# Loading part of w4 to sixteen partitions, and the last V quad with V moving, in a one-core decode block

## The chip, the core and the metric

The kernel runs on one core of a Trainium2 chip. The metric is device time in microseconds (us) of one execution; the median of three runs is given. The core has TensorE (PE; its weight loads are shown as PEld), VectorE (DVE), ScalarE (ACT), GpSimd (POOL) and SyncE (SP), which issues nearly all DMA loads here. Sixteen DMA engines move the data.

## The reference

One decode step for eight sequences (B = 8, S = 1, D = 512): attention over a window of a cache, then an MLP block, each with its residual.

```python
W = min(4096, max(256, Sk // 4))                       # 2048 of Sk = 8192
q = (layernorm(x) @ wq).reshape(B, 1, 32, 128)
k, v = the last W positions of the caches, 8 heads, each used by 4 query heads
o = softmax(q @ k^T * 128**-0.5) @ v
h = x + o.reshape(B, 1, 4096) @ wo

x = layernorm(h)
hs = token shifts of gelu(layernorm(x) @ w1) @ w2      # for S == 1 the shifts leave only zeros
x1 = x + hs
h2 = h + x1 + gelu(layernorm(x1) @ w3) @ w4            # w3: 512 x 1792, w4: 1792 x 512
```

Since S is 1, the shifted branch is zero, and w1 and w2 are not read. What is read: wq and wo (4 MB each), 32 quads of K and V (2 MB each), w3 and w4 (1.75 MB each), some 79 MB in all.

## The kernel before

Every engine has a list of operations, written out in order by the program (class `Engine`); an operation waits for the semaphore counts that it names, and counts its own engine's semaphore up. Nothing is reordered.

**The stream of loads.** `loads` lists them in order: for each sequence b and half j of the heads a K quad `("k", b, j)`, and two sequences later the V quad `("v", b, j)`, then wo in four parts, then w3 in two and w4 in four. SP issues all of them in this order. A quad is 128 partitions of 16 KB in a slot of `ring`, which has eight slots (`NS`); a load waits until the quad that held its slot has been used (`taken`). w3 lies in the slot of K quad (7, 0), w4 in that of V quad (5, 0). w4's 1792 rows are put on the 128 partitions in groups of 8, 3, 2 and 1 rows per partition (`w4_chunks`, `w4_ends`), each with a load and a semaphore of its own. FC is 14, the number of 128-row chunks of w4, and FH, 8, the number in the first group.

**Attention.** `pe_T` transposes a quarter of a K quad into `kT_ps`, ACT and DVE copy it to `kT_sb` (`evict`, L334 and L336), `pe_QK` multiplies (L345). `softmax_1` to `softmax_5` take a sequence's scores to `pT_sb`; the products with `mask_b` (L384) that spread the probabilities over head groups run on GpSimd (for the last sequence half of them on DVE). `pe_PV(i)` multiplies quarter r of V quad w = i // 4. In its form `moving` (L445) V streams through the array and the probabilities are the weights; the result holds four head groups side by side, and only a part of each is wanted: `pick_part` and `pick_rest` (L480, L483) select and add these in four steps, the first on ACT for late quads and the others on DVE, and `finish(w)` sums them with one product (L496) and scales them into `oT_all` (`scale`, L435). In its form `held` (L454), used only for the last quad (w = 15), V is the weights, 64 products accumulate the wanted result straight into `S_ps[1]`, and `scale` follows at once. NV is 15, the number of quads in the form `moving`; OWN gives quads NV - 3 and NV - 2 (12 and 13) PSUM banks of their own, and SHARE (10) is the number of quads that are picked in the main loop.

**The tail.** `reorder` (L534, L539, L540) turns `oT_all` into `oR`; `pe_wo` (L548) multiplies with the four parts of wo as they arrive. `stream(n)` (L596) is n products of 512 columns into `O2_ps` that nobody reads; such products stand between several steps. Then come the layernorm statistics (L685 to L700) and `uT` (L692), the input of w3. `pe_w3` (L710) multiplies w3 by `uT` in two halves, as its two loads arrive: eight chunks with 64 moving columns into `y_ps[0]`, six with 32 into `y_ps[1]`. DVE multiplies with `r2` (L738), ACT applies gelu (L741), `pe_fin` (L747, through `rows`) puts the residual into `z_ps`, and `pe_w4` (L755) adds the 14 chunks of w4, each as a pair of products on the two column halves, waiting for the arrival of each group. Then the copies (L775, L776) and the store.

Of the kernel before, what the change touches and what calls it, by code (L numbers as in the profile page):

```python
# [6 lines left out]
dt = mybir.dt  # L7
ACT = mybir.ActivationFunctionType
# [59 lines left out]
def bass_sequential_preLN__sliding_block_cached__mixer_s_mlp__decode_kernel(  # L68
# [23 lines left out]
    with es:  # L92
# [98 lines left out]
        sem_wo = [S(f"sem_wo{i}") for i in range(NWO)]  # L191
        sem_x, sem_wq, sem_out = (S(n) for n in ("sem_x", "sem_wq", "sem_out"))
        sem_w3 = [S(f"sem_w3{i}") for i in range(2)]
        sem_w4 = [S(f"sem_w4{i}") for i in range(4)]
# [109 lines left out]
        def landed(l, cq):  # L304
            n = place[l]
            return sem_r[n % NS], 16 * (n // NS + 1)
# [1 line left out]
        e_Tlo, e_Thi, e_lo, e_hi, e_QK, e_PV = {}, {}, {}, {}, {}, {}  # L308
        e_sp, e_max, e_mT, e_neg, e_negps, e_negc, e_exp, e_PT, e_pT, e_lsel, e_Lb, e_rL, e_scale = ({} for _ in range(13))
        NG = NB * 8  # L310
        NV = 2 * NB - 1
        LAST = NB - 1

        def split(i):
# [112 lines left out]
        OWN = {NV - 3: kbank[0], NV - 2: kbank[2]}  # L427
        banks = [O_ps[:, :], O2_ps[:, :]]

        def bank(w):  # L430
            return OWN[w] if w in OWN else banks[0] if w > NV - 2 else banks[w % 2]

        def scale(b, j, src, *waits):
            hh = slice(16 * j, 16 * (j + 1))
            e_scale[b, j] = DV.op(lambda e: e.tensor_tensor(oT_all[:, hh, b], src, rL[:, b % 4, hh], ALU.mult),  # L435
                                  e_rL[b], *waits)

        def pe_PV(i):
            b, j, r = split(i)
            s, w = place["v", b, j] % NS, i // 4  # L440

            def moving(e):
                for c in range(4 * r, 4 * r + 4):
                    t = c % 2
                    ins = e.matmul(bank(w)[64 * t:64 * (t + 1), :], pT_sb[:, b % NB3, c, 64 * j:64 * (j + 1)],  # L445
                                   ring[:, s, :].rearrange("p (a c d) -> p c a d", a=4, c=16)[:, c],
                                   start=(c < 2), stop=(c >= 14), tile_position=(0, 64 * t), skip_group_check=True)
                return ins

            def held(e):  # L450
                for c in range(16):
                    n = 16 * r + c
                    lo = 128 * c + 64 * j + 16 * r
                    ins = e.matmul(S_ps[1][:, 0:32], ring[:, s, n * DH:(n + 1) * DH],  # L454
                                   pT_sb[:, b % NB3:b % NB3 + 2].rearrange("p u c n -> p (u c n)")[:, lo:lo + 32],
                                   start=(n == 0), stop=(n == NCQ - 1))
                return ins

            if w >= NV:
                e_PV[i] = PE.op(held, landed(("v", b, j), r), e_pT[b, 3])  # L460
                taken["v", b, j] = e_PV[i]
                return
            if w in OWN:
                free = [e_lo[NG - 1], e_hi[NG - 1], e_lo[NG - 2], e_hi[NG - 2]]
            else:
                free = [e_acc[NV - 5]] if w == NV - 1 else [e_acc[w - 2] if w > 1 else None, e_xp[0]]
# [7 lines left out]
        SHARE = NV - 5  # L474
        e_part = {}

        def pick_part(w, a, eng):
# [9 lines left out]
        def pick_rest(w, *parts):  # L487
            for a in parts:
                pick_part(w, a, DV)
                if a == 3:  # L490
                    e_acc[w] = e_part[w]

        def finish(w):
            b, j = w // 2, w % 2
            hh = slice(16 * j, 16 * (j + 1))
            e_oT[w] = PE.op(lambda e: e.matmul(oT_ps[:, hh], acc[w % 3][:, :], sum_f[:, :], start=True, stop=True),  # L496
                            e_acc[w], e_sum, small[0])
            scale(b, j, oT_ps[:, hh], e_oT[w])
            small[0] = e_scale[b, j]
# [57 lines left out]
        def pv(*quarters):  # L557
            for i in quarters:
                pe_PV(i)
                if i in at:  # L560
                    finish(at[i])
                if i == NG - 1:
                    scale(LAST, 1, S_ps[1][:, 0:16], e_PV[i])

        def scores(p):
            if 0 <= p - LQK < NG:
# [26 lines left out]
        def stream(n):  # L593
            def f(e):
                for _ in range(n):
                    ins = e.matmul(O2_ps[:, :], ident_b[:, :], kT_sb[:, (NG - 1) % NKT, 0:512], start=True, stop=True)  # L596
                return ins
            if n:
                PE.op(f, e_acc[NV - 4])

        def over_exp():
            pv(49)
# [38 lines left out]
        pv(60)  # L641
        finish(14)
        pv(61, 62, 63)

        e_oR = reorder()
        stream(3)
# [19 lines left out]


        w_free = [taken[quads[n - NS]] for n in (len(quads), len(quads) + 1)]
        for a, sem in enumerate(sem_w3):
            dma(SP, w3_sb[:, 2 * a:2 * (a + 1), :].rearrange("p r f -> p (r f)"),  # L670
                B_w3[256 * a:256 * (a + 1), :].rearrange("(p r) f -> p (r f)", r=2), sem, w_free[0])

        FH = 8
        w4_chunks, w4_ends, f0 = [], [], 0
        for r, sem in zip((8, 3, 2, 1), sem_w4):
            lo = len(w4_chunks)
            w4_chunks += [slice(f0 + i, f0 + 128 * r, r) for i in range(r)]
            dma(SP, w4_sb[:, lo:lo + r, :].rearrange("p r n -> p (r n)"),
                B_w4[f0:f0 + 128 * r, :].rearrange("(p r) n -> p (r n)", r=r), sem, w_free[1] if lo == 0 else None)
            w4_ends.append(lo + r)  # L680
            f0 += 128 * r
        assert len(w4_chunks) == FC
# [22 lines left out]
        def pe_w3(half, lo, hi, *waits):  # L705
            def f(e):
                for fc in range(lo, hi):
                    n, f = divmod(fc, FH)
                    for kc in (2 * half, 2 * half + 1):
                        ins = e.matmul(y_ps[n][:, f * NY[n]:(f + 1) * NY[n]], w3_sb[:, kc, w4_chunks[fc]],  # L710
                                       uT[:, kc, 0:NY[n]], start=(kc == 0 and f == 0), stop=(kc == KC - 1),
                                       skip_group_check=True)
# [17 lines left out]
        def bcf(t, n):  # L730
            a = t[:, :]
            return bass.AP(tensor=a.tensor, offset=a.offset, ap=[a.ap[0], [0, n], [1, B]])

        e_gT = []
        for n in range(2):
            fn = (FH, FC - FH)[n]
            cs = slice(n * FH * B, (n * FH + fn) * B)
            e = DV.op(lambda e, n=n, cs=cs, fn=fn: e.tensor_tensor(v3(g_x[:, cs]),   # L738
                y_ps[n][:, 0:fn * NY[n]].rearrange("p (f w) -> p f w", w=NY[n])[:, :, 0:B], bcf(r2, fn),
                                                                   ALU.mult), e_y[n], e_r2)  # L740
            e_gT.append(AC.op(lambda e, cs=cs: e.activation(gT[:, cs], g_x[:, cs], ACT.Gelu_apprx_tanh), e))  # L741
        z_ps = S_ps[1]

        def rows(e, w, rhs, start=False, stop=False):
# [6 lines left out]
        def pe_w4(lo, hi, *waits):  # L751
            def f(e):
                for fc in range(lo, hi):
                    for a in range(2):
                        ins = e.matmul(z_ps[64 * a:64 * a + B, 0:256], gT[:, fc * B:(fc + 1) * B],  # L755
                                       w4_sb[:, fc, 256 * a:256 * (a + 1)].rearrange("p (j r) -> p r j", r=2),
                                       start=False, stop=(fc == FC - 1), tile_position=(0, 64 * a), skip_group_check=True)
                return ins
            return PE.op(f, *waits)

# [52 lines left out]
```

## Time and profile before

| | us |
|---|---|
| median of three runs (193.4 to 193.74) | 193.5 |
| the profiled execution | 193.76 |
| its span, first to last instruction | 192.3 |
| DMA busy share of the chain that ended last | 78% |
| PE, DVE, ACT, POOL busy in the span | 159.8, 103.8, 84.4, 35.8 |

The granted TensorE clock is 1.0 throughout. HBM reads are 79.18 MB, 412 GB/s over the span. The profile is a page on one execution, with a trace behind it that answers questions: a timeline of instructions, who waited for whom, groups by line, and the records of single DMA packets and semaphore arrivals. Times in a timeline count from the start of the span. A line number in it is that of the code above.

The timeline gives busy stretches as "start, length, engine, line, operation, output<-inputs, sizes, count", and in brackets how long the engine had been idle and who released it.

### The profile page before, as it was taken

Reading aid. Unit: us, or ns where it says so; the run is one execution under the profiler, and the core shown is the slowest. Engines: PE = TensorE matmul, PEld = TensorE weight load, DVE = VectorE, ACT = ScalarE, POOL = GpSimd, SP = SyncE. Lnnn points to the kernel's source line nnn. Section 1 sums busy time; section 2 is a strip of 40 time slices with the busy share of each in tenths; the row PEclk is TensorE's granted clock in tenths of the full one; section 3 lists DMA queues with packets and bytes.
Section 4 is the critical chain, followed back from the end, with each engine's and each line's share of the span. In section 5 each row is a group of like instructions: output and inputs, shape, how many; then the busy total and the mean of one; then the engine's idle time right before and its main releaser. Section 6 shows DMA issues by size and latency. Waiting matters only on the chain.

```text
span 192.3 us, 4741 instructions
## 1 busy us (share of the span) xinstructions
PE 159.8 (83%) x2108; PEld 101.8 (53%) x2108; DVE 103.8 (54%) x256; ACT 84.4 (44%) x102; POOL 35.8 (19%) x44
## 2 busy tenths in 40 slices
PE   0028999789998989998999797979998998898795
PEld 0015767567665555655656464646565653366472
DVE  7702656367457654665475546554765456552050
ACT  5002776946744544454444532454445423530040
POOL 8000000350520080008000800052004402400000
PEclk9999999999999999999999999999999999999999
DMA  6999999999999999999999999999999999999992
GB/s 220 436 423 436 433 416 433 426 428 423 436 429 433 429 433 423 426 429 431 433 423 433 429 433 429 429 433 426 424 426 429 429 433 433 423 416 430 418 381 77
DMA packets 6244, 79.47 MB, mean 413 GB/s; under 512 B 705, under 2 KB 849, under 8 KB 1361
## 3 DMA queue, kind: packets, MB, share of 16 engines
q1 hardware_dynamic: 6208, 79.18, 97.0%
q8 instruction: 16, 0.26, 0.5%
q10 hardware_dynamic: 16, 0.01, 0.0%
q14 instruction: 4, 0.02, 0.0%
HBM read 79.18 MB, written 0.01 MB: 412 GB/s over the span
## 4 chain that ended last, share of the span: by engine, by line
DMA 78%; PE 16%; DVE 2%; SPq 2%; issue 1%; ACT 0%
DMA ring<-in_A_k_cache_dram 63%; DMA ring<-in_B_w_dram 16%; PE kT_ps L325 8%; PE O_ps L445 3%; PE S_ps L345 3%; SPq L199 2%; DVE kT_sb L336 1%; PE sm L394 1%; PE sm L496 1%; DVE pT_sb L407 1%; PE S_ps L755 0%; DVE mcol L356 0%; ACT P_sb L775 0%; PE sm L360 0%; PE sm L370 0%
## 5 line engine op out<-in xcount | busy, mean ns | idle before, releaser
L334 ACT ACTIVATE kT_sb<-kT_ps 128x1024 bf16<-128x1024 bf16 x64 | 65.2, 1023 | 65.4 <-PE kT_ps L325 65.4
L325 PE MATMUL kT_ps<-ident_p,ring 128*128 128x128 bf16 x1024 | 68.3, 220 | 9.0 <-DMA ring<-in_A_k_cache_dram 7.6
L336 DVE COPY kT_sb<-kT_ps 128x1024 bf16<-128x1024 bf16 x64 | 44.3, 692 | 48.9 <-PE kT_ps L325 48.9
L325 PEld LDWEIGHTS kT_ps<-ident_p,ring 128*128 128x128 bf16 x1024 | 57.7, 98 | 22.5 <-DMA ring<-in_A_k_cache_dram 10.5
L384 POOL TENSOR_TENSOR P_sb<-P_sb,mask_b 128x512 bf16<-128x512 bf16 x30 | 31.2, 1070 | 129.2 <-ACT P_sb L374 120.1
L445 PE MATMUL O_ps<-ring,pT_sb 128*64 128x512 bf16 x208 | 31.6, 390 | 0.0
L345 PE MATMUL S_ps<-kT_sb,qwin 128*32 128x512 bf16 x256 | 26.0, 390 | 0.0
L345 PEld LDWEIGHTS S_ps<-kT_sb,qwin 128*32 128x32 bf16 x256 | 6.8, 93 | 16.3 <-issue 14.4
L394 PE MATMUL sm<-ident_s,P_sb 128*128 128x128 bf16 x120 | 11.6, 219 | 2.0 <-DVE pT_sb L407 0.7
L407 DVE COPY pT_sb<-sm 128x512 bf16<-128x512 bf16 x28 | 11.6, 415 | 1.1 <-PE sm L394 1.1
L445 PEld LDWEIGHTS O_ps<-ring,pT_sb 128*64 128x64 bf16 x208 | 7.7, 108 | 6.1 <-issue 1.6
L394 PEld LDWEIGHTS sm<-ident_s,P_sb 128*128 128x128 bf16 x120 | 7.7, 97 | 4.5 <-issue 3.6
L480 DVE SCALAR_TENSOR_TENSOR acc<-O_ps,own_f,acc 128x128 f32<-128x128 f32 x24 | 8.4, 350 | 0.8
L268 PE MATMUL S_ps<-wbig,xlnT 128*32 128x512 bf16 x32 | 3.4, 596 | 5.3 <-DMA wbig<-in_A_wq_dram 5.3
L374 ACT ACTIVATE P_sb<-S_ps,negcol 128x512 bf16<-128x512 f32 x8 | 5.5, 687 | 3.0 <-DVE negcol L373 3.0
L254 PE MATMUL sm<-ident_b,xln_b 8*128 8x8 bf16 x4 | 0.3, 174 | 7.6 <-DVE xln_b L223 7.6
L496 PEld LDWEIGHTS sm<-sum_f,acc 128*128 128x128 f32 x20 | 3.0, 188 | 6.3 <-DVE pT_sb L407 3.3
L356 DVE TENSOR_REDUCE mcol<-S_ps 128x1 f32<-128x512 f32 x8 | 5.5, 689 | 1.5 <-PE S_ps L345 1.5
L480 DVE SCALAR_TENSOR_TENSOR iota_f<-O_ps,own_f,iota_f 128x128 f32<-128x128 f32 x15 | 5.2, 348 | 1.5 <-ACT iota_f L483 1.2
L596 PE MATMUL O_ps<-kT_sb,ident_b 128*128 128x512 bf16 x21 | 5.8, 379 | 0.0
L435 DVE TENSOR_TENSOR oT_all<-sm,rL 128x16 bf16<-128x16 f32 x15 | 3.4, 229 | 4.4 <-PE sm L496 4.3
L719 ACT ACTIVATE s<-vsum,eps 128x8 f32<-128x8 f32 x1 | 0.3, 301 | 11.8 <-DVE vsum L699 11.8
(123 smaller groups left out, 109.8 us busy)
## 6 DMA issues: line engine op xcount, KB each, us to landing
ring<-in_A_k_cache_dram SPq DMA_DIRECT2D x16, 2048.0 KB, 30.7
ring<-in_A_v_cache_dram SPq DMA_DIRECT2D x16, 2048.0 KB, 26.8
wbig<-in_A_wq_dram SPq DMA_DIRECT2D x1, 4096.0 KB, 12.3
wbig<-in_A_wo_dram SPq DMA_DIRECT2D x4, 1024.0 KB, 29.9
ring<-in_B_w_dram SPq DMA_DIRECT2D x2, 896.0 KB, 34.9
ring<-in_B_w_dram SPq DMA_DIRECT2D x1, 1024.0 KB, 32.1
ring<-in_B_w_dram SPq DMA_DIRECT2D x1, 384.0 KB, 30.3
ring<-in_B_w_dram SPq DMA_DIRECT2D x1, 256.0 KB, 30.5
```

What stands on the lines that cost most here:

```text
L325: ins = e.matmul(kT_ps[m % 3][:, c * 128:(c + 1) * 128], ring[:, s, n * DH:(n + 1) * DH], ident_p[:, :], is_transpose=True)
L334: e_lo[i] = AC.op(lambda e: e.activation(kT_sb[:, i % NKT, 0:1024], kT_ps[2 * i % 3][:, :], ACT.Copy), e_Tlo[i], e_QK.get(i - NKT))
L336: e_hi[i] = DV.op(lambda e: e.tensor_copy(kT_sb[:, i % NKT, 1024:2048], kT_ps[(2 * i + 1) % 3][:, :]), e_Thi[i], e_QK.get(i - NKT))
L345: ins = e.matmul(S_ps[b % 2][32 * h:32 * (h + 1), :], qwin[:, b, 4 * j + h, w0:w0 + 32], kT_sb[:, i % NKT, :].rearrange("p (c h k) -> p h ...
L356: e_max[b] = DV.op(lambda e: e.tensor_reduce(mcol[:, :], S_ps[b % 2][:, :], AX.X, ALU.max), e_QK[8 * b + 7], e_mT.get(b - 1))
L374: e_exp[b] = AC.op(lambda e: e.activation(P_sb[:, :], S_ps[j][:, :], ACT.Exp, bias=negcol[:, j:j + 1], scale=1.0, accum_out=lcol[:, j:j + 1]),
L384: e_sp[b, r] = eng.op(lambda e, r=r, pb=pb, mb=mb: e.tensor_tensor(P4_sb[:, 128 * r:128 * (r + 1), :], pb, mb, ALU.mult), e_exp[b], e_PT.g ...
L394: ins = e.matmul(buf[:, x * 128:(x + 1) * 128], P4_sb[:, 32 * c:32 * (c + 1), :].rearrange("p k h -> p (k h)"), ident_s[:, :], is_transpos ...
L407: e_pT[b, r] = DV.op(lambda e: e.tensor_copy(dst, pT_ps[:, :]), e_PT[b, r], free)
L445: ins = e.matmul(bank(w)[64 * t:64 * (t + 1), :], pT_sb[:, b % NB3, c, 64 * j:64 * (j + 1)], ring[:, s, :].rearrange("p (a c d) -> p c a d ...
L480: e_part[w] = eng.op(lambda e: e.scalar_tensor_tensor(dst, src, own, dst, ALU.mult, ALU.add), e_part[w], e_PV[4 * w + 3])
L596: ins = e.matmul(O2_ps[:, :], ident_b[:, :], kT_sb[:, (NG - 1) % NKT, 0:512], start=True, stop=True)
```

## The change

- **128 rows of w4 apart.** Rows 0 to 127 of w4 go to `near_sb`, 64 partitions of eight rows in the slot of K quad (7, 1), of which sixteen partitions hold data (0 to 7 and 32 to 39) and the rest zeros. Eight loads bring them, each with two partitions four apart, 8 KB each, all on one semaphore `sem_near`. They stand on SP ahead of w3's loads and wait for the memset of `near_sb` on GpSimd, which waits until K quad (7, 1) is used. A second memset clears `near_w3`.
- **The other 1664 rows** go to the 128 partitions in groups of 5, 4, 3 and 1 rows per partition.
- **w3 for the near rows.** GpSimd copies the 128 columns of w3 that belong to them into `near_w3`, 64 columns wide with zeros in the rest, one copy for each of the four chunks of w3 as its half arrives. `pe_w3` has three parts now, run in the order 0, 2, 1: five chunks with 64 moving columns, eight with 32, and eight near ones (64 weight columns, 32 moving) into a third bank. DVE and ACT have three multiplications and gelus. `pe_w4` takes the near rows, eight pairs of products over 64 partitions, after the first group.
- **The last V quad** is multiplied with V moving like the others, and picked and finished like them; the form `held` is gone. NV is 16 and SHARE is NV - 6, so OWN still names quads 12 and 13, and SHARE is still 10.
- **stream(2)** ahead of w4 is gone.

```diff
-        NV = 2 * NB - 1
+        NV = 2 * NB
+        SHARE = NV - 6
...
-            if w >= NV:
-                e_PV[i] = PE.op(held, landed(("v", b, j), r), e_pT[b, 3])
-                taken["v", b, j] = e_PV[i]
-                return
...
         pv(61, 62, 63)
+        pick_rest(15, 1, 2, 3)
+        finish(15)
...
+        near_sb = ring[0:64, place["k", LAST, 1] % NS, 0:RW * D].rearrange("p (r n) -> p r n", r=RW)
+        near_w3 = ring[:, place["k", LAST, 1] % NS, RW * D:RW * D + KC * RW * 64].rearrange("p (k r n) -> p k r n", k=KC, r=RW)
+        e_nz = PO.op(lambda e: e.memset(near_sb, 0.0), taken["k", LAST, 1])
+        e_nw = PO.op(lambda e: e.memset(near_w3.rearrange("p k r n -> p (k r n)"), 0.0))
+        for n in range(RW):
+            p, f = 32 * (n // 4) + n % 4, 64 * (n // 4) + RW * (n % 4)
+            dst = near_sb[p:p + 5:4].rearrange("p r n -> p (r n)")
+            a = B_w4[f:f + RW, :]
+            dma(SP, dst, bass.AP(tensor=a.tensor, offset=a.offset, ap=[[4 * RW * D, 2], [1, RW * D]]), sem_near, e_nz)
         for a, sem in enumerate(sem_w3):
...
-        for r, sem in zip((8, 3, 2, 1), sem_w4):
+        for r, sem in zip((5, 4, 3, 1), sem_w4):
...
-        y_ps, NY = [kbank[0], kbank[2]], (64, 32)
+        y_ps, NY, PY = [kbank[0], kbank[1], kbank[2]], (64, 32, 32), (128, 64, 128)
+        e_near = [PO.op(lambda e, kc=kc: e.tensor_copy(
+            near_w3[:, kc].rearrange("p r (g n) -> p g r n", g=2)[:, :, :, 0:8],
+            w3_sb[:, kc, 0:128].rearrange("p (g n r) -> p g r n", g=2, r=RW)), (sem_w3[kc // 2], 16), e_nw)
+            for kc in range(KC)]
+        y_cols = [[lambda kc, c=c: w3_sb[:, kc, c] for c in w4_chunks[:FH]],
+                  [lambda kc, r=r: near_w3[:, kc, r, :] for r in range(RW)],
+                  [lambda kc, c=c: w3_sb[:, kc, c] for c in w4_chunks[FH:]]]
...
-        pe_w3(0, 0, FC, e_u, (sem_w3[0], 16), e_scale[LAST, 1], e_acc[NV - 2])
+        order = (0, 2, 1)
+        for n in order:
+            pe_w3(0, n, e_u, (sem_w3[0], 16), e_scale[LAST, 1], e_acc[NV - 3], e_near[1] if n == 1 else None)
         stream(1)
-        e_y = [pe_w3(1, 0, FH, (sem_w3[1], 16)), pe_w3(1, FH, FC)]
+        e_y = {n: pe_w3(1, n, (sem_w3[1], 16), *([e_near[3], (sem_near, 16 * RW)] if n == 1 else [])) for n in order}
...
-        stream(2)
         for n, hi in enumerate(w4_ends):
-            e_z = pe_w4(w4_ends[n - 1] if n else 0, hi, (sem_w4[n], 16), e_gT[0 if hi <= FH else 1])
+            e_z = pe_w4(gT, w4_sb, w4_ends[n - 1] if n else 0, hi, (sem_w4[n], 16), e_gT[0 if n == 0 else 2])
+            if n == 0:
+                pe_w4(gn, near_sb, 0, RW, e_gT[1])
```

More of the change, by code (lines that the diff above doesn't have):

```diff
@@ L193, in bass_sequential_preLN__sliding_block_cached__mixer_s_mlp__decode_kernel @@
         sem_w3 = [S(f"sem_w3{i}") for i in range(2)]
+        sem_near = S("sem_near")
         sem_w4 = [S(f"sem_w4{i}") for i in range(4)]
@@ L426, in bass_sequential_preLN__sliding_block_cached__mixer_s_mlp__decode_kernel @@
         e_acc, e_oT = {}, {}
-        OWN = {NV - 3: kbank[0], NV - 2: kbank[2]}
+        OWN = {NV - 4: kbank[0], NV - 3: kbank[2]}
         banks = [O_ps[:, :], O2_ps[:, :]]
         def bank(w):
-            return OWN[w] if w in OWN else banks[0] if w > NV - 2 else banks[w % 2]
+            return OWN[w] if w in OWN else banks[w % 2]
         def scale(b, j, src, *waits):
@@ L448, in moving @@
                 return ins
[L450 to L457, printed above, removed]
-            if w >= NV:
-                e_PV[i] = PE.op(held, landed(("v", b, j), r), e_pT[b, 3])
-                taken["v", b, j] = e_PV[i]
-                return
             if w in OWN:
@@ L465, in pe_PV @@
             else:
-                free = [e_acc[NV - 5]] if w == NV - 1 else [e_acc[w - 2] if w > 1 else None, e_xp[0]]
+                free = [e_acc[w - (4 if w >= NV - 2 else 2)] if w > 1 else None, e_xp[0]]
             e_PV[i] = PE.op(moving, landed(("v", b, j), r), e_pT[b, r], *free)
@@ L472, in pe_PV @@
                     pick_rest(w, 1, 2, 3)
-        SHARE = NV - 5
         e_part = {}
@@ L561, in pv @@
                     finish(at[i])
-                if i == NG - 1:
-                    scale(LAST, 1, S_ps[1][:, 0:16], e_PV[i])
         def scores(p):
@@ L598, in stream @@
             if n:
-                PE.op(f, e_acc[NV - 4])
+                PE.op(f, e_acc[max(w for w in e_acc if w % 2 and w not in OWN)])
         def over_exp():
@@ L671, in bass_sequential_preLN__sliding_block_cached__mixer_s_mlp__decode_kernel @@
                 B_w3[256 * a:256 * (a + 1), :].rearrange("(p r) f -> p (r f)", r=2), sem, w_free[0])
-        FH = 8
-        w4_chunks, w4_ends, f0 = [], [], 0
-        for r, sem in zip((8, 3, 2, 1), sem_w4):
+        w4_chunks, w4_ends, f0 = [], [], 128
+        for r, sem in zip((5, 4, 3, 1), sem_w4):
             lo = len(w4_chunks)
@@ L681, in bass_sequential_preLN__sliding_block_cached__mixer_s_mlp__decode_kernel @@
             f0 += 128 * r
-        assert len(w4_chunks) == FC
+        FM = FC - 1
+        FH = w4_ends[0]
+        assert len(w4_chunks) == FM
         e_uz = PO.op(lambda e: e.memset(uT, 0.0), e_PT[LAST, 3])
@@ L701, in bass_sequential_preLN__sliding_block_cached__mixer_s_mlp__decode_kernel, with pe_w3 @@
                                                       ALU.mult, ALU.add))
-        y_ps, NY = [kbank[0], kbank[2]], (64, 32)
-        def pe_w3(half, lo, hi, *waits):
+        y_ps, NY, PY = [kbank[0], kbank[1], kbank[2]], (64, 32, 32), (128, 64, 128)
[6 more added lines that the diff above has]
+                  [lambda kc, c=c: w3_sb[:, kc, c] for c in w4_chunks[FH:]]]
+        def pe_w3(half, n, *waits):
             def f(e):
-                for fc in range(lo, hi):
-                    n, f = divmod(fc, FH)
+                for f, w in enumerate(y_cols[n]):
                     for kc in (2 * half, 2 * half + 1):
-                        ins = e.matmul(y_ps[n][:, f * NY[n]:(f + 1) * NY[n]], w3_sb[:, kc, w4_chunks[fc]],
-                                       uT[:, kc, 0:NY[n]], start=(kc == 0 and f == 0), stop=(kc == KC - 1),
-                                       skip_group_check=True)
+                        ins = e.matmul(y_ps[n][0:PY[n], f * NY[n]:(f + 1) * NY[n]], w(kc), uT[:, kc, 0:NY[n]],
+                                       start=(kc == 0 and f == 0), stop=(kc == KC - 1), skip_group_check=True)
                 return ins
             return PE.op(f, *waits)
-        pe_w3(0, 0, FC, e_u, (sem_w3[0], 16), e_scale[LAST, 1], e_acc[NV - 2])
+        order = (0, 2, 1)
+        for n in order:
+            pe_w3(0, n, e_u, (sem_w3[0], 16), e_scale[LAST, 1], e_acc[NV - 3], e_near[1] if n == 1 else None)
         stream(1)
-        e_y = [pe_w3(1, 0, FH, (sem_w3[1], 16)), pe_w3(1, FH, FC)]
+        e_y = {n: pe_w3(1, n, (sem_w3[1], 16), *([e_near[3], (sem_near, 16 * RW)] if n == 1 else [])) for n in order}
         e = AC.op(lambda e: e.activation(s2[:, :], vsum[:, :], ACT.Sqrt, bias=eps2[:, :], scale=(1.0 + EPS) / D), e_vs)
@@ L728, in bass_sequential_preLN__sliding_block_cached__mixer_s_mlp__decode_kernel, with bcf @@
         e_fin = DV.op(lambda e: e.tensor_tensor(f_lo[:, :], fin[:, :], f_hi[:, :], ALU.subtract), e)
-        def bcf(t, n):
-            a = t[:, :]
+        def bcf(t, n, p):
+            a = t[0:p, :]
             return bass.AP(tensor=a.tensor, offset=a.offset, ap=[a.ap[0], [0, n], [1, B]])
[L734 to L741, printed above, removed]
+        gn_x = P4_sb[0:64, 96:128, :].rearrange("p k h -> p (k h)").bitcast(dt.float32)
+        gn = P4_sb[0:64, 64:80, :].rearrange("p k h -> p (k h)")
+        halves = [slice(0, FH * B), slice(FH * B, FM * B)]
+        g_parts = [(g_x[:, halves[0]], gT[:, halves[0]]), (gn_x, gn), (g_x[:, halves[1]], gT[:, halves[1]])]
+        e_gT = {}
+        for n in order:
+            gx, g = g_parts[n]
+            fn = len(y_cols[n])
+            y = y_ps[n][0:PY[n], 0:fn * NY[n]].rearrange("p (f w) -> p f w", w=NY[n])[:, :, 0:B]
+            e = DV.op(lambda e, gx=gx, y=y, fn=fn, n=n: e.tensor_tensor(v3(gx), y, bcf(r2, fn, PY[n]), ALU.mult), e_y[n], e_r2,
+                      e_PT[LAST, 3])
+            e_gT[n] = AC.op(lambda e, gx=gx, g=g: e.activation(g, gx, ACT.Gelu_apprx_tanh), e)
         z_ps = S_ps[1]
@@ L749, in rows, with pe_w4 @@
             return ins
-        def pe_w4(lo, hi, *waits):
+        def pe_w4(g, w, lo, hi, *waits):
             def f(e):
@@ L754, in f @@
                     for a in range(2):
-                        ins = e.matmul(z_ps[64 * a:64 * a + B, 0:256], gT[:, fc * B:(fc + 1) * B],
-                                       w4_sb[:, fc, 256 * a:256 * (a + 1)].rearrange("p (j r) -> p r j", r=2),
-                                       start=False, stop=(fc == FC - 1), tile_position=(0, 64 * a), skip_group_check=True)
+                        ins = e.matmul(z_ps[64 * a:64 * a + B, 0:256], g[:, fc * B:(fc + 1) * B],
+                                       w[:, fc, 256 * a:256 * (a + 1)].rearrange("p (j r) -> p r j", r=2),
+                                       start=False, stop=(w is w4_sb and fc == FM - 1), tile_position=(0, 64 * a), skip_group_check=True)
                 return ins
```

## The prediction

> **What bounds the kernel now.** I read the page first (busy slices, the DMA line, the chain), then the timeline from 148 us to the end, then the trace's records of single DMA packets and of single semaphore arrivals. From the page:
>
> ```profile
> DMA  6999999999999999999999999999999999999992
> ...
> ## 4 chain that ended last, share of the span: by engine, by line
> DMA 78%; PE 16%; DVE 2%; SPq 2%; issue 1%; ACT 0%
> ```
>
> The transfers are busy in every slice but the first and the last, and hold 78% of the chain. The last slices decide. The timeline of the tail (start, busy time, instruction):
>
> ```profile
> 181.36 0.97 PE L548 MATMUL S_ps<-oR,wbig 128*128 128x32 bf16 x32 [0.75 <-DMA wbig<-in_A_wo_dram]
> ...
> 183.53 1.46 PE L710 MATMUL kT_ps<-P_sb,ring 128*128 128x64 bf16 x28
> ...
> 185.57 1.45 PE L710 MATMUL kT_ps<-P_sb,ring 128*128 128x64 bf16 x28 [0.36 <-DMA ring<-in_B_w_dram]
> ...
> 187.99 0.77 PEld L755 LDWEIGHTS S_ps<-ring,gT 128*8 128x8 bf16 x16 [0.59 <-DMA ring<-in_B_w_dram]
> ...
> 189.20 0.21 PEld L755 LDWEIGHTS S_ps<-ring,gT 128*8 128x8 bf16 x6 [0.44 <-DMA ring<-in_B_w_dram]
> 189.82 0.09 PEld L755 LDWEIGHTS S_ps<-ring,gT 128*8 128x8 bf16 x4 [0.41 <-DMA ring<-in_B_w_dram]
> 190.13 0.09 PEld L755 LDWEIGHTS S_ps<-ring,gT 128*8 128x8 bf16 x2 [0.22 <-DMA ring<-in_B_w_dram]
> 190.45 0.45 ACT L775 ACTIVATE P_sb<-S_ps 8x256 bf16<-8x256 f32 x1 [2.91 <-PE S_ps L755]
> ```
>
> TensorE waits for a transfer at each stage: the last part of wo, the second half of w3, all four parts of w4. It has 0.75 us to spare before the last wo products and 0.2 to 0.4 us at each later step. So two ends compete: the last arrival of w4 and TensorE's own list.
>
> The records of arrivals show a skew. The sixteen increments of the last w4 load land in two bunches: seven from 186.66 to 187.42, one at 188.33, eight from 189.61 to 190.09. Following each engine's packets, which run back to back, the late eight are those that twice served a 16 KB instruction fetch (the 16 packets of q8), each of which set an engine back by about 1.4 us.
>
> **The transfers after.** In the records an 8 KB packet takes 306 ns, 3 KB 118, 2 KB 80, 1 KB 43, so 37.6 ns per further KB; 5 KB is then about 193 and 4 KB 156. An engine carries eight packets of each load. Before: 8×(306+118+80+43) = 4.38 us of w4; after, without the 128 rows: 8×(193+156+118+43) = 4.08 us. Fourteen engines save 0.30 us. The rows themselves: x_sb's load of eight rows shows eight data packets and eight arrivals, so I take a load of two partitions to use two engines, and all eight such loads the same two, which gain 8×306 ns = 2.45 us, net 2.15. If both are early ones (187.42 + 2.15 = 189.57), the last arrival is that of the late bunch: 189.91 - 0.30 = 189.61. The one at 190.09 is late by the last fetch, 0.92 us at 187.05, during the last w4 loads; TensorE's list is longer afterwards, so this fetch falls behind that engine's last packet or its bunch. Arrivals alone give -0.48 us.
>
> **The waits on SP and GpSimd.** The eight loads wait for a memset on GpSimd, and behind them on SP stand w3 and w4. GpSimd ends its last products of P_sb at 165.26; the memset of 4096 elements, by qwin's (3840 in 3.29 us), ends at 168.8, the second one (2048) at 170.5, then uT's, not read before 183.3. SP issues 14 loads at about 0.45 us: w3 is out by 173, all by 175.1. The first engine ends wo at 178.0, so four microseconds cover this; were the cover gone, every microsecond would be one of the total. Costed at nothing.
>
> **The last V quad.** Timeline before:
>
> ```profile
> 171.65 0.55 PE L454 MATMUL S_ps<-pT_sb,ring 128*128 128x32 bf16 x16
> ...
> 172.24 0.40 PE L496 MATMUL sm<-sum_f,iota_f 128*128 128x16 f32 x2
> ...
> 172.48 1.35 PE L454 MATMUL S_ps<-pT_sb,ring 128*128 128x32 bf16 x48
> ...
> 173.87 0.23 DVE L435 TENSOR_TENSOR oT_all<-S_ps,rL 128x16 bf16<-128x16 f32 x1 [0.97 <-PE S_ps L454]
> ...
> 174.15 0.42 PE L534 MATMUL kT_ps<-oT_all,pick 128*32 128x64 bf16 x32 [0.32 <-DVE oT_all L435]
> ```
>
> Removed: 64 products and a direct scale. Added: 16 products (pairs every 0.216 us at L445), one ACT and three DVE picks, a sum on TensorE. Twelve of the products start at 172.48; eight took 1.10 us from first start to the ACT pick (169.56 to 170.66), so twelve take 1.53: ACT at 174.01. From that pick to finish's product took 1.57 (170.66 to 172.23): 175.58. To the scale 0.44: 176.02 against 173.87. The reorder moves from 174.15 to 176.30, the first wo products from 175.80 to 177.95: +2.15. From there TensorE runs 64 products (1.60), four unread ones (0.86), 32 (0.80), four more (0.86): the last wo part starts at 182.07 instead of 181.36. So 1.44 of the 2.15 goes into idle time, +0.71 stays. The first half of w3 moves from 183.53 to 184.24. GpSimd's copies into near_w3 start at 183.4 and may hold up DVE just here: L415, 0.23 us elsewhere, took 0.75 beside GpSimd's products and ended with them (164.54 to 165.29). One copy of 128 elements is 0.2 to 0.35 us; bounds 0 to 0.35, I take 0.1: 184.34.
>
> **The tail on TensorE.** In the first half, products moving 64 columns start every 60 ns and those moving 32 every 25. Now 10×60 + 16×25 = 1.00 us, then 16 products of the near rows, with 64 weight columns, a form that before does not show. The nearest rows are 25 ns (same moving width) and 60 ns; I take 30, so 0.48. A change of array shape also shows: from the last w3 product to the first of L747, which writes a column half, 0.106 us instead of 0.025; from L747 to the unread products 0.152. I take 0.1 per change, bounds 0 to 0.15. First half: 1.00 + 0.48 + 0.2 = 1.68 to 186.02, the unread product 0.215: 186.24 (the load landed at 185.52, no longer waited for; before, 185.57). Second half 1.58: 187.82. The eight products of L747: 0.25, so w4 begins at 188.07; its first part landed at 187.1 (185.52 + 8×193 ns) and the first gelu is long done. Its products go in pairs every 0.1135 us: 21 pairs instead of 14, with two changes of shape around the 64-partition near rows. The last pair starts at 188.07 + 20×0.1135 + 0.2 = 190.54; none of its loads is later (189.61). The copies start 0.32 after the last pair (190.134 to 190.454): 190.86 against 190.45. The rest is unchanged. Sum: +0.4. With every unknown at its low end (25 ns, no changes of shape, no hold-up) it is 190.3, -0.15; with all at the high end (60 ns and 0.15) about 192, +1.5. Taking out the two unread products before w4 saves 0.43 us of TensorE, already in this.
>
> [...]
>
> **The rivals.**
> One: the two engines are late ones. Then w3's second half lands at 185.52 + 2.45 = 187.97 and the tail hangs from there: 187.97 - 186.24 = +1.73 on top of 0.4, +2.1 (195.6); the last arrival, 189.91 + 2.15, is hidden behind that. Against: of the eight engines that x_sb's load used, two are late, so a blind pair is clean in 15 of 28. [...] Chance 0.14.
> Two: one of them is the engine at 188.33. Its w3 part lands at 183.94 + 2.45 = 186.4, its last at 190.47; either way +0.4 to 0.6 (194.0). Chance 0.10.
> Three, on the other side: TensorE keeps up (unread products and near products overlap better than I have it) and the arrivals decide: 189.61 + 0.05 + 0.32 = 189.98, -0.47 (193.05). For: all low ends already give -0.15. Against: it needs 0.3 us more. Chance 0.18, the part of the low ends near it included.
> Should the loads spread over all sixteen engines after all, the arrivals end about where they did, at 190.0, and TensorE's list still ends later; this lies in my forecast.
>
> **How the numbers follow.** The sum stands against the profiled execution, 193.76 us (span 192.3), which is 0.26 above the median, 193.5. Between the low end (-0.15) and the sum (+0.4) I stay nearer to the sum, since the changes of shape are read from rows: +0.3, that is 193.8 by the median. This case has 0.58; within it 0.33 is less than 0.2% (0.39 us, about what a measurement of this kernel can tell from no change) and 0.25 more. Slower: 0.25 + 0.14 + 0.10 = 0.49; same 0.33; faster 0.18. The likeliest case alone spans 193.35 to 194.9; the range 193.0 to 194.9 adds the third rival and the second, and leaves the first out.
>
> **What would show it.** Right: reorder near 176.3, the last wo products starting near 182.1 with no transfer before them, w3's halves at 184.3 and 186.2, w4's products without idle time from 188 on, final arrivals by 189.6. Wrong: waits for a transfer still before the last w4 products (three), or before w3's second half with arrivals after 187 (one).

## The result and the profile after

| | before, us | after, us |
|---|---|---|
| median of six runs each | 193.44 (193.37 to 193.74) | 194.61 (194.19 to 194.99) |
| the profiled execution | 193.76 | 194.99 |
| its span | 192.3 | 193.5 |
| DMA / PE share of the chain that ended last | 78% / 16% | 62% / 29% |

The ratio is 1.0057, 95% interval 1.0043 to 1.0072: slower by 1.1 us (0.8 to 1.4), where 0.3 was forecast. The ratios and intervals of this document leave out the few executions that took over 1.5% longer than the fastest of the same kernel (some of e7, e8 and e11).

The clock row of the page before, and from the page after the clock row, the DMA row (forty slices of the span) and the chain:

```profile
PEclk9999999999999999999999999999999999999999
```

```profile
PEclk9999999999999999999999999999999999998799
DMA  6999999999999999999999999999999999999980
...
DMA 62%; PE 29%; DVE 5%; issue 1%; SPq 1%; ACT 1%
```

The transfers now die out ahead of the last slice, TensorE's share of the chain has nearly doubled, and the clock row has an 8 and a 7 that the row of before had not. The tail of the same execution, TensorE's products and the first copy (start, length, instruction, in brackets the idle time ahead and its releaser):

```profile
172.66 1.49 PE L447 MATMUL O_ps<-ring,pT_sb 128*64 128x512 bf16 x12
...
175.76 0.39 PE L484 MATMUL sm<-sum_f,acc 128*128 128x16 f32 x2 [1.62 <-DVE acc L468]
...
176.48 0.42 PE L522 MATMUL kT_ps<-oT_all,pick 128*32 128x64 bf16 x32 [0.32 <-DVE oT_all L437]
...
178.13 1.87 PE L536 MATMUL S_ps<-oR,wbig 128*128 128x32 bf16 x64 [0.48 <-DVE oR L528]
180.21 1.36 PE L582 MATMUL O_ps<-kT_sb,ident_b 128*128 128x512 bf16 x3 [0.22 <-issue]
181.41 0.95 PE L536 MATMUL S_ps<-oR,wbig 128*128 128x32 bf16 x32
...
183.08 0.95 PE L536 MATMUL S_ps<-oR,wbig 128*128 128x32 bf16 x32
...
185.24 1.65 PE L715 MATMUL kT_ps<-P_sb,ring 128*128 128x64 bf16 x42
...
187.05 1.62 PE L715 MATMUL kT_ps<-P_sb,ring 128*128 128x64 bf16 x42
...
188.82 0.73 PE L765 MATMUL S_ps<-ring,gT 128*8 128x256 bf16 x10
...
191.60 0.45 ACT L786 ACTIVATE P_sb<-S_ps 8x256 bf16<-8x256 f32 x1 [2.39 <-PE S_ps L765]
```

No wait for a transfer is left from 176 us to the end; before there were seven. The reorder is at 176.48 (forecast 176.30), the last wo products are at 183.08 (forecast 182.07), and from the first half of w3 (185.24) on all is one unbroken list. From the first wo products (178.13) to the third part of wo (181.41) it takes 3.28 us where the forecast has 2.46, so 0.8 us is lost there. The same stretch by windows (columns: stretch, its length, busy us of PE, PEld, DVE, ACT, POOL with counts, granted TensorE clock, DMA share, GB/s):

```profile
174.00:175.00 1.00, 0.14 (x2) 0.00 (x0) 0.38 (x2) 0.80 (x2) 0.00 (x0) 1.00 0.97 410
175.00:176.00 1.00, 0.24 (x2) 0.24 (x2) 0.67 (x2) 0.85 (x1) 0.00 (x0) 1.00 1.03 434
176.00:177.00 1.00, 0.57 (x34) 0.47 (x35) 0.25 (x2) 0.00 (x0) 0.00 (x0) 1.00 1.04 442
177.00:178.00 1.00, 0.59 (x2) 0.10 (x1) 0.94 (x2) 0.00 (x0) 0.00 (x0) 0.95 0.98 415
178.00:179.00 1.00, 0.87 (x33) 0.90 (x34) 0.00 (x0) 0.00 (x0) 0.00 (x0) 0.50 1.00 422
179.00:180.00 1.00, 0.99 (x38) 0.94 (x36) 0.00 (x0) 0.00 (x0) 0.00 (x0) 0.50 1.01 426
180.00:181.00 1.00, 0.79 (x2) 0.30 (x2) 0.00 (x0) 0.00 (x0) 0.00 (x0) 0.50 0.99 416
181.00:182.00 1.00, 1.00 (x26) 0.74 (x25) 0.00 (x0) 0.00 (x0) 0.00 (x0) 0.84 1.06 444
```

While ACT and DVE pick the last quad (174 to 176), TensorE has almost nothing to do; then the granted clock is 0.50 from 177.90 to 181.32 (0.95 in the 177 window is 0.1 us of it, 0.84 in the 181 window 0.32). In that time the 512-column unread products start 0.43 us apart instead of 0.215. The chain of the forecast had no such term.

Theory: both halves of the change lengthen TensorE's list, the new gap makes its clock fall over the wo products (a fall is a stretch at half the granted clock), and the list then decides the end. Rivals: one half of the change alone costs it; or the tail costs more than the sum has.

### The profile page after: what moved, and what is told of

It reads as the page before. It is cut to its first block, busy times and chain, and to the rows that moved or that the text cites. A ratio compares the mean times of both kernels' runs of the same rounds, so it can differ in the third digit from the quotient of the medians.

```text
span 193.5 us, 4747 instructions
## 1 busy us (share of the span) xinstructions
PE 160.6 (83%) x2098; PEld 102.5 (53%) x2102; DVE 105.0 (54%) x260; ACT 85.1 (44%) x104; POOL 42.5 (22%) x50
## 4 chain that ended last, share of the span: by engine, by line
DMA 62%; PE 29%; DVE 5%; issue 1%; SPq 1%; ACT 1%
DMA ring<-in_A_k_cache_dram 62%; PE kT_ps L327 8%; PE O_ps L447 6%; PE S_ps L347 3%; PE O_ps L582 2%; PE S_ps L536 2%; PE sm L484 2%; PE kT_ps L715 2%; DVE kT_sb L338 1%; PE S_ps L765 1%; PE kT_ps L447 1%; PE sm L396 1%; SPq L200 1%; DVE P_sb L386 1%; DVE acc L468 1%
## 5 line engine op out<-in xcount | busy, mean ns | idle before, releaser
L447 PE MATMUL O_ps<-ring,pT_sb 128*64 128x512 bf16 x224 | 33.7, 390 | 0.0
L447 PEld LDWEIGHTS O_ps<-ring,pT_sb 128*64 128x64 bf16 x224 | 8.4, 108 | 7.0 <-issue 1.6
L468 DVE SCALAR_TENSOR_TENSOR acc<-O_ps,own_f,acc 128x128 f32<-128x128 f32 x27 | 9.5, 350 | 2.4 <-ACT acc L471 1.6
L484 PE MATMUL sm<-sum_f,acc 128*128 128x16 f32 x22 | 4.3, 273 | 3.3 <-DVE acc L468 1.6
L582 PE MATMUL O_ps<-kT_sb,ident_b 128*128 128x512 bf16 x15 | 4.8, 422 | 0.4 <-issue 0.4
```

Of the source, the lines that this page charges most:

```text
L468: e_part[w] = eng.op(lambda e: e.scalar_tensor_tensor(dst, src, own, dst, ALU.mult, ALU.add), e_part[w], e_PV[4 * w + 3])
```

## The experiments

Times are medians against the kernel before on the same chip (193.46 to 193.57 in the three sets).

**e1, the quad held again.** After, with the last quad as before; only the near rows are left.

```diff
-        NV = 2 * NB
+        NV = 2 * NB - 1
...
-        pick_rest(15, 1, 2, 3)
-        finish(15)
```

> The change with its last part undone: the last V quad is multiplied in the form held again, everything else as in the changed kernel. Theory (TensorE's list sets the end, and the loss comes from the detour of the last V quad and the clock that drops behind it): reorder near 174.2, the last wo products at 181.4, w3's first half at 183.5, the second at the arrival (185.8), w4 from 187.6; copies near 190.4; 193.4 us, as before, within 0.3. Rival (the loads of the near rows, or the near products, cost it): at least 194.2 remains, with a transfer or near products ahead of an idle TensorE.

Measured: 194.18, ratio 1.0038 (1.002 to 1.0056), but this is no middle: six executions lie at 193.54 to 193.70 and six at 194.66 to 194.95. The lower ones are what the theory expects. The profiled one is an upper one; its clock is 1.0 from 174 to 191 and its wo and w3 are early, yet TensorE stops amid the near products, where the profile names no wait (1.05 us between two weight loads, 0.75 without a product):

```profile
187.48 0.74 PE L778 MATMUL S_ps<-ring,gT 128*8 128x256 bf16 x10
188.14 0.61 PE L778 MATMUL S_ps<-ring,P_sb 64*8 64x256 bf16 x7
189.51 0.73 PE L778 MATMUL S_ps<-ring,P_sb 64*8 64x256 bf16 x9 [0.75 <-issue]
```

**e2, the moving form alone.** Before, with the last quad as in the change and nothing else.

```diff
-        NV = 2 * NB - 1
+        NV = 2 * NB
...
+        pick_rest(15, 1, 2, 3)
+        finish(15)
```

> The kernel before with one part of the change alone: the last V quad with V moving, picked and finished like the others. Theory: the same gap and clock drop as in the changed kernel, the first half of w3 near 185.2, w4's 14 pairs from 188.9, copies 190.75: +0.3, 193.75 us; the near rows then stand for the other 0.8 to 0.9. Rival (the detour is the whole loss): +1.2, 194.6. Rival (the detour is hidden by the transfers): 193.4.

Measured: 193.62, ratio 1.0012 (1.0003 to 1.0021). The reorder is at 176.50 and the clock falls here too, in this execution from 176.25 to 179.66, most of it ahead of the wo products (178.32); the last wo part starts at 182.55. With before's shorter tail this costs 0.16, where I expected 0.3.

**e3, the gap filled.** After, with seven unread products between the last quad's products and its sum.

```diff
         pick_rest(15, 1, 2, 3)
+        def fill(e):
+            for _ in range(7):
+                ins = e.matmul(S_ps[1][:, :], ident_b[:, :], kT_sb[:, (NG - 1) % NKT, 0:512], start=True, stop=True)
+            return ins
+        PE.op(fill, e_exp[LAST])
         finish(15)
```

> The changed kernel with seven unread products of 512 columns put into TensorE's gap ahead of the sum of the last V quad. Theory (the gap lets the granted clock fall to 0.5, and the unread products behind it then take 0.43 us each): the clock stays at 1.0, the second pair of wo parts starts 0.9 earlier, 193.7 us. Rival (the clock does not fall because of this gap, or falls without costing anything): 194.6, unchanged or later by what the products push back.

Measured: 194.18 (194.02 to 194.32), ratio 1.0034 (1.0022 to 1.0046): 0.4 below the kernel after, the way that was expected of the clock, but 0.5 above the 193.7 that I gave. Its timeline:

```profile
176.42 0.42 PE L522 MATMUL kT_ps<-oT_all,pick 128*32 128x64 bf16 x32 [0.32 <-DVE oT_all L437]
...
180.53 0.96 PE L536 MATMUL S_ps<-oR,wbig 128*128 128x32 bf16 x32
...
182.20 0.95 PE L536 MATMUL S_ps<-oR,wbig 128*128 128x32 bf16 x32
...
184.35 1.66 PE L721 MATMUL kT_ps<-P_sb,ring 128*128 128x64 bf16 x42
...
187.95 0.73 PE L771 MATMUL S_ps<-ring,gT 128*8 128x256 bf16 x10
```

The clock stays at 1.0 from 173 to 183, the reorder comes when it did, and every later step lies where the prediction put it: 182.20 (182.07), 184.35 (184.34), 187.95 (188.07), copies 190.73 (190.86). Adding work to the idle engine made the kernel faster. It is the times that show this: all five executions lie at 194.02 to 194.32, while nine of the eleven of the kernel after lie at 194.38 or above (e9). The profile alone would not, since in that of e5 the clock holds without the filling.

**e4, no unread products between the parts of wo.**

```diff
-            stream((0, 4, 4, 1)[n])
+            stream((0, 0, 0, 1)[n])
```

> The changed kernel without the unread products behind the second and the third part of wo (eight of 512 columns). Theory (TensorE's list sets the end, so work taken out of it comes back in full until a transfer is the limit): the last wo products start at the arrival of wo, 181.3, instead of 183.1: -1.7 us until w3's second half (185.8) limits, so about -1.2: 193.4 us, if the clock holds in the pauses this opens; with a clock of 0.5 in w3 and w4, 195 or more. Rival (transfers set the end): unchanged, 194.6.

Measured: 193.65, ratio 1.001 (1.0001 to 1.0019). The clock falls all the same (178.32 to 181.72 in its profile), but TensorE's list is shorter by 1.7 us there and meets the transfers again:

```profile
181.22 1.00 PE L536 MATMUL S_ps<-oR,wbig 128*128 128x32 bf16 x32 [0.53 <-DMA wbig<-in_A_wo_dram]
...
185.60 1.66 PE L715 MATMUL kT_ps<-P_sb,ring 128*128 128x64 bf16 x42 [0.19 <-DMA ring<-in_B_w_dram]
```

So it is TensorE's list that costs the time, not the new loads. I expected 193.4; from the second half of w3 on (185.60) TensorE's list still runs to the end without a wait for a transfer.

**e5, the unread products ahead of w4 put back.**

```diff
         PE.op(pe_fin, e_fin, e_exp[LAST], e_scale[LAST, 1])
+        stream(2)
```

> After, with the two unread products put back ahead of the first part of w4 (0.215 us each at full clock). Theory: in the changed kernel TensorE works without a wait from the second half of w3 to the end, so its list sets the end and the two products are paid in full: 194.61 + 0.43 = 195.04 us, the copies 0.4 later. Rival: something else (an arrival or a gelu) still ends the tail, and the products fall into its wait: 194.6.

Measured: 195.31 (194.67 to 195.73), ratio 1.0096 (1.0082 to 1.0111), some 0.7 above after, with four executions. Paid at least in full: the list sets the end. The profiled execution has no fall in the tail, though its gap is the unfilled 1.62 us (its one fall is from 117.98 to 121.40, amid the attention): 194.67, which is 0.5 above the sum without a fall, 194.17. From the last residual products to w4 it has 0.75 us, after has 0.11, so the step takes 0.64 and not only the 0.43 of two products.

**After again (e9).** No edit.

> The changed kernel itself once more, to see each execution's time beside its mean granted clock. Theory: without the fall of the clock the time is that of the sum, 194.17 (as the execution at clock 1.0, 194.19, and e3); with it, it lies at 194.4 to 195.0, by how much of the fall's 3.4 us lies over work; some 194.6 as median. Rival: the spread has another cause, and executions at clock 1.0 lie at 194.6 as well.

Measured: 194.43 (194.19 to 194.96), ratio 1.0052 (1.004 to 1.0064). All eleven executions of the changed kernel, with the mean granted clock of each (one fall of 3.41 us takes 0.009 from it, wherever in the span it lies):

| mean clock | times, us |
|---|---|
| 1.000 | 194.19, 194.19 |
| 0.991 | 194.43, 194.65, 194.77, 194.96, 194.99 |
| 0.982 | 194.38, 194.39, 194.57, 194.58 |

Without a fall the kernel takes 194.19 both times. The nine others lie 0.2 to 0.8 higher. The mean clock doesn't tell where a fall was: the profile of this run (0.982) has two, one from 118.28 to 121.69 and one from 176.31 to 179.72, and the profiles of e3 (0.991, 194.05) and e5 have only one of the first kind, which cost nothing that shows. So the 0.2 to 0.8 are put down to falls in the tail, of which two were profiled. The one of this run lies more over waiting than that of the first profile: the last wo part starts at 182.64 instead of 183.08.

**e10, three products in the gap instead of seven.**

> As e3, with three unread products (0.65 us) in the gap ahead of the last quad's sum instead of seven. Theory: what counts is how busy TensorE is over some 3.4 us, so a gap of about 0.9 us, shorter than others that left the clock at 1.0, is enough: 194.2 as e3, clock 1.0. Rival: any idle time at this place lets the clock fall in some executions: 194.2 to 194.7, as mixed as the changed kernel.

Measured: 194.27 (193.97 to 195.01), ratio 1.0045 (1.0032 to 1.0058). Five executions have clock 1.0 (193.97 to 194.49), one 0.991 (195.01). That one was profiled; the fall is from 178.12 to 181.54. So the theory's number holds for most, and "enough" was wrong. TensorE's busy time in the 3.42 us ahead of the fall (or in a like stretch without one), first the kernel after, then e10, e3 and e5:

```profile
174.48:177.90 3.42, 1.41 (x36) 0.81 (x37) 2.17 (x6) 1.36 (x2) 0.00 (x0) 1.00 1.01 428
```

```profile
174.70:178.12 3.42, 1.75 (x41) 0.91 (x41) 2.06 (x6) 1.07 (x1) 0.00 (x0) 1.00 1.01 426
```

```profile
174.50:177.90 3.40, 2.61 (x42) 1.16 (x41) 2.22 (x6) 1.28 (x1) 0.00 (x0) 1.00 1.03 437
```

```profile
174.00:177.42 3.42, 1.33 (x36) 0.81 (x37) 1.84 (x6) 1.65 (x2) 0.00 (x0) 1.00 1.01 426
```

Falls followed 1.41 and 1.75 us of work, none followed 2.61, but none followed the 1.33 of e5 either. So it isn't any 3.42 us that count, and that the work over 3.4 us decides was not shown. The clock records of the traces show which stretches may count: all twelve falls that end within a profile last 3.41 us, and what lies between two changes of the clock is each time a whole multiple of that (in after, 3.413 us at 0.50 and then 13.653 at 1.00, four times as long; in e9 and e2 two falls begin 58.03 us apart, 17 times 3.413). My estimate from these records is that in one execution all changes lie on such steps. Carried on from its one fall, the steps of e5 are at 172.60 and 176.01: TensorE was busy for 1.78 us between them and then for 2.46 us, and the clock held; ahead of six of the seven falls in the tail it was busy for 1.31 to 1.75 us, ahead of the seventh (e8) for 2.81. The steps of e3, worked out in the same way, lie within 0.1 us of e5's, which is why its profile doesn't show by itself that the seven products kept the clock.

**e6 and e11, the stop of e1.** e1 with 95, and with 12, unread products of 8 columns at the start, which push all later instructions back in TensorE's list.

```diff
+        def early(e):
+            for _ in range(95):   # e11: 12
+                ins = e.matmul(O2_ps[:, 0:8], ident_b[:, :], ident_b[:, 0:8], start=True, stop=True)
+            return ins
+        PE.op(early, e_idb)
```

> The kernel of e1 (near rows, last quad in the held form) with 95 unread products of 8 columns added at the start, where TensorE waits for wq until 13 us. They move every later instruction by 190 places in TensorE's instruction stream, and change nothing else. Theory: the stop of 1.02 us amid the near products is TensorE waiting for its own instructions, at a boundary of the 16 KB fetches (some 124 products apart): the boundary falls behind the last product and all executions lie at 193.5 to 193.7, where half of e1's were. If the boundary shows up elsewhere, it is some 95 products earlier, in the first half of w3. Rival: the stop belongs to what runs at that moment (the near products, the transfers): half of the executions stay at 194.7 to 194.95, with the stop where it was.

> e1 with 12 unread products of 8 columns at the start (24 places in TensorE's instruction stream; e6 had 190 and so one instruction fetch more). Theory: the stop of 1.02 us is at a fixed place of the instruction stream, so it moves to 12 products earlier, amid the first group of w4; the executions stay in two groups, 193.6 and 194.8. Rival: the stop is tied to the near products: it stays between their seventh and ninth. If the last fetch falls elsewhere in time, the two groups become one.

e6: 194.58 (194.50 to 194.71), ratio 1.0052 (1.004 to 1.0064), one group. Its near products run without a stop, but it has a 17th 16 KB instruction fetch (before and after have 16, the row "q8 instruction: 16, 0.26, 0.5%" of their pages), and one engine's packets of w4 land 1.3 us behind the others (at 190.98; the rest by 189.70), so that TensorE waits 0.55 and 0.31 us for them. This misses the expected 193.6 for a reason of its own. e11: 193.50 to 196.60, five executions below 193.73 and seven above 195.1. In its profile (an upper one) the stop has moved:

```profile
187.51 0.50 PE L784 MATMUL S_ps<-ring,gT 128*8 128x256 bf16 x5
189.50 0.50 PE L784 MATMUL S_ps<-ring,gT 128*8 128x256 bf16 x5 [1.48 <-issue]
189.93 1.07 PE L784 MATMUL S_ps<-ring,P_sb 64*8 64x256 bf16 x16
```

In e1 it came after ten and seven products of w4, in e11 after five: twelve earlier, so at the same place of TensorE's list, behind its 2086th product. In both it ended at 189.5, 2.3 to 2.4 us after the start of a 16 KB instruction fetch (187.16 and 187.12). That TensorE waits there for its instructions is my reading of two profiles: they name no releaser ("issue"), and why only some of the executions stop is open. The kernels before and after have 2071 and 2064 products and don't reach the place: the stop is no part of the result. It does leave the near rows alone measured by only part of the executions, six of twelve in e1 and five of twelve in e11.

**e7 and e8, a shorter list.** e4, without the unread product between the halves of w3, and with 32 moving columns in all of w3; e8 has e3's seven products as well.

```diff
-        y_ps, NY, PY = [kbank[0], kbank[1], kbank[2]], (64, 32, 32), (128, 64, 128)
+        y_ps, NY, PY = [kbank[0], kbank[1], kbank[2]], (32, 32, 32), (128, 64, 128)
...
-        stream(1)
         e_y = {n: pe_w3(1, n, (sem_w3[1], 16), ...
```

> After, without the unread products between the parts of wo (as e4) and between the halves of w3, and with 32 moving columns instead of 64 in the first five chunks of w3 (10 products per half at about 25 instead of 40 ns). Theory: with w4 begun by 187.25 TensorE meets the last arrivals (189.55), and these decide: copies at 189.55 + 0.06 + 0.32 = 189.93, that is 193.3 us, 0.15 below the kernel before. Rival: TensorE stays the bound, the moving columns matter little: 193.6 as e4.

> e7 with the seven unread products of e3 ahead of the last quad's sum. Theory: with the short list the fall of the clock after that gap lies ahead of the last arrival of wo and costs nothing, so the same as e7, 193.3 us, with the clock at 1.0 throughout. Rival: the fall still reaches the last part of wo or w3 in some executions: e8 is 0.1 to 0.3 us below e7 and scatters less.

e7: 193.47 to 193.75 in six executions at a mean clock of 0.991, 195.90 to 196.53 in six at 0.969 to 0.978. e8: 193.46 and 193.55 at 1.0, 194.76 and 194.92 at 0.991 and 0.982, four at 196.06 to 196.42 below. The ratios are 1.0046 (1.0011 to 1.0081) and 1.0075 (1.0036 to 1.0114). Both expectations failed. The profile of e8 (194.76) shows one way:

```profile
185.00:186.00 1.00, 0.47 (x12) 0.42 (x11) 0.90 (x4) 0.98 (x1) 0.41 (x2) 0.86 1.01 415
186.00:187.00 1.00, 1.00 (x29) 0.96 (x27) 0.72 (x4) 0.29 (x2) 0.37 (x2) 0.50 0.80 321
187.00:188.00 1.00, 1.00 (x22) 0.96 (x22) 0.22 (x1) 0.30 (x2) 0.00 (x0) 0.50 0.71 279
```

The clock falls at 185.72 (0.86 in the 185 window is 0.28 us of it), over the part of the tail where every delay counts; that less work ahead of w3's second half brings this on is argued and not shown. The profile of e7 (193.75) has its fall from 177.60 to 181.01, ahead of the last part of wo, where it costs nothing. By the 0.009 that one fall takes, I estimate two to four falls in each of the six slower executions (0.969 to 0.978); none of them was profiled. The narrower columns brought nothing either: the first ten products of a half start 40 ns apart with 64 moving columns (after) and with 32 (e7). No version beat the kernel before.

## Why the prediction was right in sign and short in size

- **Transfers: right.** Of the last load, eight increments land from 189.28 to 189.87 and five from 186.46 to 186.85; the two engines of the near rows are early ones, their last increments at 188.34 to 188.84 with those of a third. The last arrival is 189.87, forecast 189.61 (190.09 in the kernel before); w3's second half lands at 185.79 (185.52 in the kernel before). Rivals one and two did not occur. Two late engines of the eight that x_sb's load used give rival one a chance of 13 in 28; no run shows what would lower that to the 0.14 of the forecast, and the profile of after shows only that the two engines were early ones.
- **SP and GpSimd: right, nothing lost.** The memsets end at 168.77 and 170.52 (168.8 and 170.5). SP is 1.5 us later with its last load than I had it (176.64), still ahead of its engines.
- **The last quad: right up to the reorder.** ACT's pick 174.18, the sum 175.76, the reorder 176.48: each 0.17 or 0.18 later than forecast, as the twelve products already are (172.66 for 172.48).
- **From the reorder to the last wo part: the step that failed.** "From there TensorE runs 64 products (1.60), four unread ones (0.86), 32 (0.80), four more (0.86)" takes the full clock. It held in e3, with 4.13 us from the first wo product (178.07) to the last part, forecast 4.12, and in e5's profile without the filling (177.98 to 182.10); in the profile of after it took 4.95. I counted the new idle time, 1.62 us as measured, only as time, not as what it may do to the clock. In the profile of after the granted clock was 0.50 for 3.41 us (177.90 to 181.32), behind 3.42 us in which TensorE was busy for 1.41; what makes it fall is not isolated by any run.
- **GpSimd's hold-up of DVE: absent.** The copies ran from 183.70 to 184.44, before DVE's L690 at 184.99. The term was 0.1.
- **The tail: right within 0.15.** From the first w4 product to the copies 2.78 us, forecast 2.79; shape changes 0.107 to 0.115 us at the near rows of w3 (0.1). The stretch from w3 to w4 is 3.58, forecast 3.73. The near products of w3 start 32 ns apart (30); each half of w3 took 0.03 to 0.1 us less than the sum, since 64-column products take 40 and not 60 ns. I had read 60 as the price of 64 moving columns; e7 shows that it isn't. What sets it is not isolated; it goes with the step between the weight columns (60 ns at a step of 8 in before; in after 40 at 5, some 33 at 4, 25 to 29 at 3 and less).
- **From the sum to the median: the second error.** The sum was 193.76 + 0.41 = 194.17, and 194.19 is what the kernel takes without a fall. I then took off 0.26, because the median of before was so much below its profiled execution, and 0.11 towards the low end. But before ends by its last arrival, and its profiled execution had a late one (190.09); after ends by TensorE, which an earlier arrival does not help. That the other executions of before had earlier arrivals is inferred, since only one was profiled. The low end was also added up wrongly: without any change of shape, those around the near rows of w4 included, the prediction's own terms give 190.10 for the copies (-0.35), not 190.3 (-0.15). And that 194.17 meets 194.19 so closely is in part luck: the absent hold-up (0.1) and the shorter stretch from w3 to w4 (0.15) are offset by wo products that begin 0.1 to 0.2 late in the profiles of e3 and after.

Together: 193.8 + 0.11 + 0.26 = 194.17, and 0.4 for the fall gives 194.6. The same count explains the halves: alone, the moving form costs 0.16 and the near rows 0.13 (e1's lower group, median 193.59; not the 0.8 to 0.9 that I gave them in e2), since each fits into the idle time ahead of the arrivals; together they use it up.

## What to carry to other kernels

A change that moves the end from the transfers to an engine makes that engine's sum an absolute time: set it against the profiled execution, and not against a median that other arrivals may have set. Before taking work off TensorE, or putting a wait in front of it, look at how much it does in the 3.4 us around: here six of the seven falls in the tail came behind 1.31 to 1.75 us of work in 3.41. Products that nobody reads may be what keeps its clock: e3, with seven more of them, took 194.02 to 194.32, where nine of the eleven executions of after lie at 194.38 or above. Judge this by many executions: across the same gap of 1.62 us the clock held in the profile of e5 and fell in that of after. Two edits that are each hidden by the same idle time are not hidden together (0.16 and 0.13 alone, 1.1 together).

## What the hardware showed that was not expected

- In the tail the clock fell when TensorE had been busy for 1.31 to 1.75 of the 3.41 us ahead, around a gap of 0.87 us at the least (e10), but not in every execution: by the mean clock, one of six in e10 and nine of eleven in after had a fall somewhere. Within each profile its changes lie whole multiples of 3.41 us apart. In e8 it fell after a stretch that the profile counts as 2.81 of 3.41 us busy, most of it 32-column products, and in e5 it held after 1.78; busy time alone does not tell.
- TensorE stopped for 0.75 us (e1) and 1.48 us (e11) behind the same product of its list, the 2086th, and went on 2.3 to 2.4 us after the start of a 16 KB instruction fetch; that it waited for this fetch is a reading of two profiles. In e6, which has one fetch more, one engine's last packets came 1.3 us late (190.98, the rest by 189.70). So 12 and 95 products put in at the start changed where the tail stopped or what it waited for.
